# A planner that brings VectorE's planned time up to TensorE's at every unit of products

## The chip, the cores and the metric

The kernel runs on one core of a Trainium2 chip. Five engines work side by side on that core: TensorE (PE in the profile; PEld is its weight load), VectorE (DVE), ScalarE (ACT), GpSimd (POOL) and SyncE (SP), which here only issues transfers. Each engine has its own list of instructions, and semaphores make one wait for another. The metric is the device time of one execution in microseconds (us), lower is better; runs of the kernel before agree within 0.1%.

## The reference

The input goes through a block-wise linear attention with decay, then through two gated feed-forward layers. In short:

```python
for b in range(nb):                       # blocks of 64 positions
    intra = (qb @ kb.T * Dmask) @ vb
    inter = (qb * lam_pow) @ kv_state
    out[b] = intra + inter
    kv_state = lam_block * kv_state + (kb * rev_pow).T @ vb
x = out.reshape(1536, 512)
h = x @ w_in1;  x = (h * clip(h + 3, 0, 6) / 6) @ w_out1      # first layer, 512 -> 2048 -> 512
h = max(x @ w_in2, 0);  return (h * h) @ w_out2               # second layer, the same sizes
```

The four weight matrices arrive in 64-bit floating point; q, k, v and lam are 32-bit.

## The kernel before

**Tiles.** After the attention the 1536 tokens lie in three blocks of 512 (`j` = 0 to 2). The 2048 hidden features of a layer are 16 tiles of 128 (`f`), handled in four groups of four (`GROUP`). A *hidden unit* (`hidden`, called "h") multiplies one block by one tile of the input weights; a *projection unit* (`project`, called "y") multiplies a group's four hidden tiles of a block by the output weights for one quarter of the result, and adds the group's part to an accumulator. Every value is split into a high and a low part, so a product takes three matmuls: each unit is 12 matmuls of 128x512.

**The order of the units.** A list written at the end of the function sets it. For each layer, group and block it puts one hidden unit, then the four projection units of the block before, then the three other hidden units of the group. Around the change's place, in the second layer (`layer` 1), this reads: h of block 0 tile 4; four y of block 2, group 0; h of block 0 tiles 5, 6, 7; h of block 1 tile 4; four y of block 0, group 1; h of block 1 tiles 5, 6, 7.

**What follows a hidden unit in the second layer.** ScalarE reads the product `ph` from PSUM and applies Relu (L410), squares it (L411) and writes the high part `gh` (L412); VectorE subtracts that to get the low part `gl` (L414). (The slots of these two have other names for some tiles: `gkT` and `gk`, `gv` and `gq`, `gA`.) Three PSUM buffers hold `ph`, so a hidden unit can begin only when ScalarE has read the one three hidden units before. A projection unit takes the group's tiles in turn; the 12th of its matmuls takes the low part of the fourth tile. For group 0 the result is copied by ScalarE (L462); for later groups VectorE adds it to the accumulator (L465).

**Decoding of the weights.** A tile of 64-bit weights is fetched by SyncE into one of four `raw` buffers (L136). ScalarE takes a magnitude `da` (L145), VectorE then makes seven pieces of work: clamp (L160), shift (L164), join (L170), power (L177), lower (L181), rest (L186) and add (L189). After join ScalarE writes the high part (`wih` or `woh`, L173), for which rest waits; add writes the low part (`wil` or `wol`). There are seven places for decoded tiles of each kind, and a tile's place becomes free when its last product is done: for `w_out` of a group, after the last projection unit of block 2.

**The planner.** All engines' orders are those in which the Python code calls the instructions. The code keeps two planned times, `pe_t` for TensorE and `dve_t` for VectorE. A unit adds 2.72 to `pe_t` and then calls `decode_until(pe_t)`, which puts in pieces of decoding, at 0.44 or 0.7 each, until `dve_t` is 0.3 past `pe_t`. `vector(ready, cost)` does the same up to the time at which a piece of the products' own VectorE work is ready, and then counts that work; a subtraction `gl` of the second layer is called for `pe_t` + 2.4. Two things let `dve_t` stand still while `pe_t` goes on: `decode_piece` returns 0 when no place for a decoded tile is free, and a projection unit of group 0 calls no `vector`, since ScalarE copies its result.

Of the kernel before, what the change touches and what calls it, by code (L numbers as in the profile page):

```python
# [33 lines left out]
def decay_attention_moe_moe(  # L34
# [175 lines left out]
    pe_t, dve_t = 0.0, 0.0  # L210
    freed = []

    def decode_until(us):
        nonlocal dve_t
        while dve_t < us + LATE:
            cost = decode_piece()
            if not cost:
                return
            dve_t += cost
# [4 lines left out]
        dve_t = max(dve_t, ready) + cost  # L224

    def unit():
        nonlocal pe_t
        pe_t += UNIT
        decode_until(pe_t)

# [156 lines left out]
    def hidden(layer, j, f):  # L387

        n = BLOCKS[j] * P
        free_weights()  # L390
        wih, wil = weight(("wi", layer, f))
        ph = ps_h.tile([P, n], F32, tag="ph", name="ph")
        for a in range(KD):
            for i, (w, x) in enumerate(((wih, x_hi[j]), (wih, x_lo[j]), (wil, x_hi[j]))):
                nc.tensor.matmul(  # L395
                    ph, w[:, a * P : (a + 1) * P], x[:, a, :],
                    start=a == 0 and i == 0, stop=a == KD - 1 and i == 2,
                )
        if j == len(BLOCKS) - 1:
            freed.append(("wi", layer, f))  # L400
        unit()
        s, gh, gl = g_tiles()
        gh, gl = gh[:, :n], gl[:, :n]
        g = gp.tile([P, n], F32, tag="g", name="g")
        if layer == 0:
            nc.scalar.activation(g, ph, AF.Relu, bias=three)  # L406
            vector(pe_t + SCALAR, TWO)
            nc.vector.scalar_tensor_tensor(g, g, 6.0, ph, op0=ALU.min, op1=ALU.mult)  # L408
        else:
            nc.scalar.activation(g, ph, AF.Relu)  # L410
            nc.scalar.activation(g, g, AF.Square)  # L411
        nc.scalar.copy(gh, g)  # L412
        vector(dve_t + SCALAR if layer == 0 else pe_t + 3 * SCALAR, TWO)
        nc.vector.tensor_tensor(gl, g, gh.bitcast(F32), op=ALU.subtract)  # L414
        g_t[layer, j, f] = (gh, gl, s)
# [13 lines left out]
    def project_by_unit(layer, j, grp, f):  # L429

        n = BLOCKS[j] * P
        free_weights()
        if f == GROUP * grp:
            two = ps_s.tile([P, 2, n], F32, tag="sc", name="py2")
            py_t.update({e: two[:, e, :] if e < 2 else ps_y.tile([P, n], F32, tag="py", name="py") for e in range(KD)})
        for e in range(KD):
            products(layer, j, grp, e, f, py_t[e])
        unit()
        if f == GROUP * (grp + 1) - 1:
            for e in range(KD):  # L440
                project(layer, j, grp, e, py_t.pop(e))

    def project(layer, j, grp, e, py=None):
# [4 lines left out]
        if py is None:  # L448
            free_weights()
            py = ps_y.tile([P, w], F32, tag="py", name="py")  # L450
            for f in fs:
                products(layer, j, grp, e, f, py)
            unit()
# [67 lines left out]
    dve_t = 1.0  # L521
# [66 lines left out]
```

## Time and profile before

| | |
|---|---|
| median of 3 runs | 585.89 us (585.48 to 586.01) |
| the profiled execution | 587.42 us, of which its span 585.6 us |
| TensorE busy | 572.7 us, 98% of the span |
| VectorE busy | 420.4 us, 72% |
| ScalarE busy | 255.5 us, 44% |
| mean granted TensorE clock | 0.993 |

The span runs from the first to the last instruction; 1.8 us of the profiled execution lie around it. Engines overlap, so the shares don't add up. A TensorE instruction is shown with its whole passage through the array (0.39 us), while the next one starts 0.227 us after it: gaps are read from the starts. A number in square brackets behind a row of a timeline is how long the engine had been idle, and what ended that.

### The profile page before, as it was taken

How to read it: one execution, taken by the hardware profiler on the slowest of the kernel's cores; microseconds unless marked ns; L12 is line 12 of the kernel's file. 1: busy time of each engine (PE TensorE's matmuls, PEld its weight loads, DVE VectorE, ACT ScalarE, POOL GpSimd, SP SyncE). 2: the span in 40 equal slices, each digit the busy share in tenths (PEclk: the TensorE clock that was granted, in tenths of full speed). 3: DMA queues.
4: the chain of work that ended last, by engine and by line, in shares of the span. 5: the costliest groups of instructions: out<-in, count | busy, mean ns of one | idle time of the engine just before them, and what ended most of it. 6: DMA issues, size and time to landing. Idle time of an engine off the chain costs nothing.

```text
span 585.6 us, 7733 instructions
## 1 busy us (share of the span) xinstructions
PE 572.7 (98%) x3022; PEld 471.1 (80%) x3022; DVE 420.4 (72%) x723; ACT 255.5 (44%) x417; POOL 31.6 (5%) x36
## 2 busy tenths in 40 slices
PE   8899999999999999999999999988999999999997
PEld 5788888888888888888888888876888888888885
DVE  6789899989885899579988993379543998242222
ACT  1224555453441443344554774454522654532530
POOL 3782000000000000000000000000000000000000
PEclk9999999999999999999999999998999999999999
DMA  8982223332230232112221331113110320001011
GB/s 324 407 313 74 72 73 107 109 107 78 67 109 4 73 105 73 36 39 70 73 72 37 108 114 67 37 72 109 36 37 0 99 82 1 0 1 54 37 54 72
DMA packets 18035, 49.77 MB, mean 85 GB/s; under 512 B 2128, under 2 KB 2128, under 8 KB 18000
## 3 DMA queue, kind: packets, MB, share of 16 engines
q1 hardware_dynamic: 17856, 49.04, 24.0%
q8 instruction: 23, 0.38, 0.3%
q10 hardware_dynamic: 144, 0.26, 0.1%
q14 instruction: 12, 0.10, 0.1%
HBM read 46.14 MB, written 3.15 MB: 84 GB/s over the span
## 4 chain that ended last, share of the span: by engine, by line
PE 93%; DVE 3%; DMA 3%; ACT 0%; issue 0%; SPq 0%; DVEq 0%
PE py L427 45%; PE ph L395 43%; PE pxt L330 2%; PE psc L314 2%; PE pxt L355 1%; DMA lent<-in_qT 1%; DMA lent<-in_k 1%; PE pst L336 1%; DMA k<-in_k 1%; DVE du L186 0%; DVE da L181 0%; ACT da L145 0%; DVE du L170 0%; DVE wil L189 0%; DVE da L177 0%
## 5 line engine op out<-in xcount | busy, mean ns | idle before, releaser
L395 PE MATMUL ph<-xh,wih 128*128 128x512 f32 x384 | 149.6, 390 | 1.8 <-ACT g L410 1.8
L395 PE MATMUL ph<-xh,wil 128*128 128x512 f32 x384 | 149.4, 389 | 0.0
L395 PE MATMUL ph<-xl,wih 128*128 128x512 f32 x384 | 149.4, 389 | 0.0
L465 DVE TENSOR_TENSOR acc<-acc,py 128x512 f32<-128x512 f32 x72 | 49.3, 685 | 51.3 <-PE py L427 50.7
L395 PEld LDWEIGHTS ph<-xh,wih 128*128 128x128 f32 x384 | 72.1, 188 | 17.2 <-ACT g L410 2.2
L395 PEld LDWEIGHTS ph<-xh,wil 128*128 128x128 f32 x384 | 72.1, 188 | 15.0
L395 PEld LDWEIGHTS ph<-xl,wih 128*128 128x128 f32 x384 | 72.1, 188 | 15.0
L145 ACT ACTIVATE da<-raw 128x512 f32<-128x512 f32 x64 | 43.0, 674 | 42.4 <-DVE wol L189 22.5
L414 DVE TENSOR_TENSOR gl<-g,gh 128x512 fp32r<-128x512 f32 x48 | 33.0, 687 | 38.7 <-ACT gh L412 38.6
L410 ACT ACTIVATE g<-ph 128x512 f32<-128x512 f32 x48 | 28.6, 597 | 59.8 <-PE ph L395 59.8
L181 DVE SCALAR_TENSOR_TENSOR da<-raw,da 128x512 f32<-128x512 uint32 x64 | 44.6, 696 | 2.0
L170 DVE SCALAR_TENSOR_TENSOR du<-raw,da 128x512 int32<-128x512 int32 x64 | 44.3, 691 | 2.0
L173 ACT CAST woh<-du 128x512 fp32r<-128x512 f32 x32 | 19.8, 620 | 59.0 <-DVE du L170 59.0
L408 DVE SCALAR_TENSOR_TENSOR g<-g,ph 128x512 f32<-128x512 f32 x48 | 32.9, 685 | 14.5 <-ACT g L406 14.3
L412 ACT CAST gh<-g 128x512 fp32r<-128x512 f32 x48 | 29.9, 623 | 21.1 <-DVE g L408 20.4
L427 PE MATMUL py<-woh,gl 128*128 128x512 f32 x96 | 37.8, 394 | 0.0
L427 PE MATMUL py<-wol,gh 128*128 128x512 f32 x96 | 37.7, 392 | 0.0
L406 ACT ACTIVATE g<-ph,three 128x512 f32<-128x512 f32 x48 | 32.9, 686 | 10.8 <-PE ph L395 10.3
L427 PE MATMUL py<-woh,gh 128*128 128x512 f32 x96 | 37.6, 392 | 0.0
L427 PE MATMUL py<-gh,woh 128*128 128x512 f32 x96 | 37.3, 389 | 0.0
L427 PE MATMUL py<-gl,woh 128*128 128x512 f32 x96 | 37.3, 389 | 0.0
L427 PE MATMUL py<-gh,wol 128*128 128x512 f32 x96 | 37.3, 389 | 0.0
(94 smaller groups left out, 913.9 us busy)
## 6 DMA issues: line engine op xcount, KB each, us to landing
raw<-in_w_in SPq DMA_DIRECT2D x32, 512.0 KB, 3.2
raw<-in_w_out SPq DMA_DIRECT2D x32, 512.0 KB, 3.3
out<-acc SPq DMA_DIRECT2D x12, 256.0 KB, 2.0
kT<-in_kT SPq DMA_DIRECT2D x6, 256.0 KB, 5.2
k<-in_k SPq DMA_DIRECT2D x6, 256.0 KB, 5.1
v<-in_v SPq DMA_DIRECT2D x6, 256.0 KB, 5.3
lent<-in_kT SPq DMA_DIRECT2D x6, 256.0 KB, 5.4
lent<-in_qT SPq DMA_DIRECT2D x6, 256.0 KB, 5.4
```

The lines of the kernel that those rows point to most:

```text
L145: nc.scalar.activation(abs_t[n], raw_t[n][:, :, 1].bitcast(F32), AF.Abs, scale=2.0**16)
L170: nc.vector.scalar_tensor_tensor(u, hi32, -(2**31), ai, op0=ALU.bitwise_and, op1=ALU.bitwise_or)
L173: nc.scalar.copy(hi, u.bitcast(F32))
L181: nc.vector.scalar_tensor_tensor(a, lo32.bitcast(U32), 2.0**-52, a, op0=ALU.mult, op1=ALU.mult)
L395: nc.tensor.matmul(ph, w[:, a * P : (a + 1) * P], x[:, a, :], start=a == 0 and i == 0, stop=a == KD - 1 and i == 2,)
L406: nc.scalar.activation(g, ph, AF.Relu, bias=three)
L408: nc.vector.scalar_tensor_tensor(g, g, 6.0, ph, op0=ALU.min, op1=ALU.mult)
L410: nc.scalar.activation(g, ph, AF.Relu)
L412: nc.scalar.copy(gh, g)
L414: nc.vector.tensor_tensor(gl, g, gh.bitcast(F32), op=ALU.subtract)
L427: nc.tensor.matmul(py, a, b, start=f == fs[0] and i == 0, stop=f == fs[-1] and i == 2)
L465: nc.vector.tensor_tensor(t, t, py, op=ALU.add)
```

## The change

One line is added to `unit()`, which every hidden and projection unit calls once: before it adds the unit's 2.72 to `pe_t`, `dve_t` is raised to `pe_t` if it is below. Nothing else is edited; from there on the line numbers are one higher.

```diff
     def unit():
-        nonlocal pe_t
+        nonlocal pe_t, dve_t
+        dve_t = max(dve_t, pe_t)
         pe_t += UNIT
         decode_until(pe_t)
```

The orders of PE, POOL and SP are the same before and after. VectorE's and ScalarE's differ in one stretch, in the second layer, from the first hidden unit behind block 2's projection units of group 0 up to the projection units of block 1 in group 1. No instruction is added or left out.

VectorE before, at the start of that stretch: `wih3` and `wih4` are decoded input weights, `gl3` is the low part of block 0's tile 5. Ahead of the first row shown stand the whole decoding of `woh2`, and of `wih3` all but its last two pieces.

```order
L186 TENSOR_TENSOR du_3387<-du_3387,wih3_786 128x512
L189 TENSOR_TENSOR wil3_787<-du_3387,da_3376 128x512
L160 TENSOR_SCALAR da_3389<-da_3389 128x512
L164 TENSOR_SCALAR da_3389<-da_3389 128x512
L170 SCALAR_TENSOR_TENSOR du_3400<-raw_3188,da_3389 128x512
L177 TENSOR_SCALAR da_3389<-du_3400 128x512
L181 SCALAR_TENSOR_TENSOR da_3389<-raw_3188,da_3389 128x512
L186 TENSOR_TENSOR du_3400<-du_3400,wih4_1125 128x512
L189 TENSOR_TENSOR wil4_1126<-du_3400,da_3389 128x512
L160 TENSOR_SCALAR da_3402<-da_3402 128x512
L164 TENSOR_SCALAR da_3402<-da_3402 128x512
L414 TENSOR_TENSOR gl3_870<-g_3409,gh3_869 128x512
```

VectorE now, at the same place: `gl3`, `gk` and `gq` are the low parts of block 0's tiles 5, 6 and 7. Ahead of the first row stand the same decoding of `woh2` and the clamp and shift of `wih3`.

```order
L170 SCALAR_TENSOR_TENSOR du_3391<-raw_3110,da_3376 128x512
L415 TENSOR_TENSOR gl3_870<-g_3384,gh3_869 128x512
L177 TENSOR_SCALAR da_3376<-du_3391 128x512
L181 SCALAR_TENSOR_TENSOR da_3376<-raw_3110,da_3376 128x512
L186 TENSOR_TENSOR du_3391<-du_3391,wih3_786 128x512
L415 TENSOR_TENSOR gk_945<-g_3412,gkT_944 128x512
L189 TENSOR_TENSOR wil3_787<-du_3391,da_3376 128x512
L160 TENSOR_SCALAR da_3393<-da_3393 128x512
L164 TENSOR_SCALAR da_3393<-da_3393 128x512
L170 SCALAR_TENSOR_TENSOR du_3440<-raw_3188,da_3393 128x512
L415 TENSOR_TENSOR gq_1020<-g_3433,gv_1019 128x512
```

So `gl3` stands behind 10 pieces of decoding instead of 23, and three or four pieces stand between one low part and the next.

ScalarE before, behind the four copies of block 2's projection units: two magnitudes and two casts of input weights stand ahead of the Relu (L410) of block 0's tile 5.

```order
L173 CAST woh2_997<-du_3374 128x512
L145 ACTIVATE da_3389<-raw_3188 128x512
L173 CAST wih3_786<-du_3387 128x512
L145 ACTIVATE da_3402<-raw_3215 128x512
L173 CAST wih4_1125<-du_3400 128x512
L410 ACTIVATE g_3409<-ph_3361 128x512
L411 ACTIVATE g_3409<-g_3409 128x512
L412 CAST gh3_869<-g_3409 128x512
```

ScalarE now, at the same place (Relu is L411):

```order
L173 CAST woh2_997<-du_3374 128x512
L411 ACTIVATE g_3384<-ph_3361 128x512
L412 ACTIVATE g_3384<-g_3384 128x512
L413 CAST gh3_869<-g_3384 128x512
L145 ACTIVATE da_3393<-raw_3188 128x512
L173 CAST wih3_786<-du_3391 128x512
```

The Relu of tile 5 now comes ahead of these casts. The decoding of `wih4`, `wih5` and of `woh3` to `woh5` moves back in the same way, until the two orders meet again in the four additions (L465, now L466) of block 1 in group 1.

## Rows read from the trace of the kernel before

**Rows 1.** The page's first part: engines' busy time, share, instructions.

```profile
PE 572.7 (98%) x3022; PEld 471.1 (80%) x3022; DVE 420.4 (72%) x723; ACT 255.5 (44%) x417; POOL 31.6 (5%) x36
```

**Rows 2.** The chain that ended last: start, us, what it was.

```profile
337.99 10.88 PE ph L395 x48
...
370.63 10.89 PE py L427 x48
...
581.48 0.69 DVE acc L465
```

**Rows 3.** Timeline of PE, 370 to 410 us: start, us, instruction [idle before].

```profile
370.25 0.39 PE L395 MATMUL ph<-xh,wil 128*128 128x512 f32 x1
...
381.35 0.39 PE L395 MATMUL ph<-xh,wih 128*128 128x512 f32 x1
...
389.29 0.39 PE L395 MATMUL ph<-xh,wil 128*128 128x512 f32 x1
391.50 0.50 PE L395 MATMUL ph<-xh,wih 128*128 128x512 f32 x1 [1.82 <-ACT g L410]
...
395.95 0.39 PE L427 MATMUL py<-wol,gkT 128*128 128x512 f32 x1
397.26 0.50 PE L427 MATMUL py<-woh,gk 128*128 128x512 f32 x1 [0.92 <-DVE gk L414]
...
398.04 0.40 PE L427 MATMUL py<-wol,gv 128*128 128x512 f32 x1
399.26 0.50 PE L427 MATMUL py<-woh,gq 128*128 128x512 f32 x1 [0.82 <-DVE gq L414]
...
409.38 0.39 PE L395 MATMUL ph<-xh,wih 128*128 128x512 f32 x1
```

**Rows 4.** Windows: from:to, us, busy (instructions) by engine, granted clock, DMA share, GB/s.

```profile
25.40:27.30 1.90, 0.03 (x2) 0.00 (x0) 1.90 (x4) 1.10 (x2) 0.00 (x0) 1.00 1.02 402
27.30:31.80 4.50, 4.46 (x54) 3.90 (x56) 3.38 (x5) 0.00 (x0) 3.43 (x3) 0.62 1.05 403
...
399.80:403.50 3.70, 3.70 (x11) 2.89 (x10) 3.63 (x8) 1.11 (x3) 0.00 (x0) 0.54 0.40 117
```

**Rows 5.** Timeline of ACT, 366 to 412 us.

```profile
370.67 0.60 ACT L410 ACTIVATE g<-ph 128x512 f32<-128x512 f32 x1 [0.80 <-PE ph L395]
...
381.55 0.59 ACT L462 COPY acc<-py 128x512 f32<-128x512 f32 x1 [2.13 <-PE py L427]
...
382.60 0.61 ACT L173 CAST woh<-du 128x512 fp32r<-128x512 f32 x1
...
390.33 0.62 ACT L173 CAST wih<-du 128x512 fp32r<-128x512 f32 x1 [0.85 <-DVE du L170]
390.85 0.59 ACT L410 ACTIVATE g<-ph 128x512 f32<-128x512 f32 x1
```

**Rows 6.** Timeline of DVE, 340 to 412 us.

```profile
342.73 0.69 DVE L414 TENSOR_TENSOR gl<-g,gh 128x512 fp32r<-128x512 f32 x1
...
345.72 0.68 DVE L414 TENSOR_TENSOR gq<-g,gv 128x512 fp32r<-128x512 f32 x1
...
372.62 0.69 DVE L414 TENSOR_TENSOR gl<-g,gh 128x512 fp32r<-128x512 f32 x1 [2.03 <-ACT gh L412]
...
383.24 0.69 DVE L186 TENSOR_TENSOR du<-du,woh 128x512 f32<-128x512 f32 x1 [7.21 <-ACT woh L173]
...
384.64 0.42 DVE L160 TENSOR_SCALAR da<-da 128x512 f32<-128x512 f32 x1
...
388.69 0.42 DVE L160 TENSOR_SCALAR da<-da 128x512 f32<-128x512 f32 x1
...
393.52 0.68 DVE L414 TENSOR_TENSOR gl<-g,gh 128x512 fp32r<-128x512 f32 x1
...
398.52 0.68 DVE L414 TENSOR_TENSOR gq<-g,gv 128x512 fp32r<-128x512 f32 x1
```

**Rows 7.** DMA issues on the page: instructions, KB each, median us to landing.

```profile
raw<-in_w_out SPq DMA_DIRECT2D x32, 512.0 KB, 3.3
```

## The prediction

> **What bounds the kernel now.** I read the page's busy times first, then the chain of waits, then the timelines of TensorE, ScalarE and VectorE around the one place where the order changes, and the windows for the granted clock. TensorE is busy for 572.7 of 585.6 us, VectorE for 420.4 [rows 1]. The chain says the same: from the first hidden unit on it is made of pieces of TensorE, 10.88 us for 48 matmuls (0.2267 us each, 2.72 us a unit) [rows 2]. VectorE can thus cost time only where TensorE waits for it, and what the change is worth must be read at the stretch that it rearranges.
>
> That stretch is where the chain leaves TensorE. The 96 matmuls from the first of block 0's tile 5 (381.35) to the first of block 1's tile 5 (409.38) take 28.03 us [rows 3]; at 0.2267 each they would take 21.76. The loss is 6.27 us, and its parts are seen in the starts:
> - 389.29 to 391.50: the hidden unit of block 1 waits for ScalarE's Relu, which frees a `ph` buffer; 2.21 less a matmul's 0.23 is 1.98 us [rows 3].
> - 395.95 to 397.26: TensorE waits for VectorE's `gk`, the low part of tile 6; 1.08 us [rows 3].
> - 398.04 to 399.26: it waits for `gq`, that of tile 7; 0.99 us [rows 3].
> - 399.80 to 403.50: TensorE runs on, but the granted clock is 0.54, near the lower of its two levels; 3.70 times 0.46 is 1.70 us [rows 4].
> - The other 0.52 us are single intervals a little over 0.2267 behind each gap.
>
> Why it happens stands in the other two timelines. VectorE is idle for 7.21 us until 383.24, since the cast of `woh` that it waits for stands behind four copies on ScalarE, the last at 381.55 [rows 5, 6]. The planner counted no such standstill: its `dve_t` had stayed behind while no place was free and ScalarE did the copies, so it thought that VectorE had had those units for decoding, and put 23 pieces ahead of tile 5's low part. They run from 383.24 on without a pause, and the low part comes at 393.52 [rows 6]. ScalarE is drawn in: its Relu stands behind casts that wait for VectorE's join, the last at 390.33, and so begins at 390.85, though its matmuls began their last at 381.35 + 11 x 0.2267 = 383.84 [rows 3, 5].
>
> **The change part by part.** No instruction comes or goes, and TensorE's and the DMA queue's orders stay, so all of it is this one rearrangement. I carry it forward from the same 381.35.
>
> *The lag without a queue.* A last matmul at 370.25 is followed by the Relu at 370.67 and the low part at 372.62, 0.69 long [rows 3, 5, 6]. So a Relu follows by 0.42, and the low part by 1.95 more.
>
> *Tile 5.* Relu at 384.26: ScalarE is free, its cast of `woh` ends at 382.60 + 0.61 = 383.21 [rows 5]. Its low part would be ready at 386.2. VectorE has the clamp, shift and join of `wih3` ahead of it, from 384.64; seven pieces take 388.69 - 384.64 = 4.05 us, 0.58 each, so it is free at 386.4 [rows 6]. The low part begins there, against 393.52. The `ph` buffer is free at about 384.9, and the unit that waits for it comes at 381.35 + 3 x 2.72 = 389.51: the 1.98 us go.
>
> *Tile 6.* Its last matmul begins at 386.56, but now a magnitude and a cast stand ahead of its Relu, behind tile 5's high part (386.2): some 1.2 us by rows of 0.6 each [rows 5], so Relu at 387.4 and low part at 389.4. TensorE wants it as the 9th matmul of the unit at 392.23, at 394.04: 4 us in hand less the 0.7 that it takes. The 1.08 us go.
>
> *Tile 7.* Last matmul 389.28, Relu 389.7, ready at 391.6. VectorE has four pieces between the two low parts, 390.1 + 2.3 = 392.4, and ends at 393.1. It is wanted as the 12th matmul, 392.23 + 2.49 = 394.72: 1.6 us in hand. The 0.99 us go. This is the tightest place here.
>
> *What is late next.* The work put off is decoding, `wih4` and `wih5`, then `woh3` to `woh5`; those weights belong to group 2, which TensorE reaches only after two more rounds of 8 units, 40 us on, so their own lateness costs nothing. What it could cost is lateness of block 1's low parts, which before had VectorE almost to themselves. There, from 403.11 on, a low part (0.6) with four pieces (2.3) makes 2.9 us on VectorE for each unit of 2.72: it falls back 0.2 us a unit, 0.8 in four units, against 1.6 to 2.4 in hand. The trace has a near likeness: at 342.73 and 345.72 two low parts stand 2.99 us apart with four pieces of output weights between them, and TensorE's 48 matmuls from 337.99 still take 10.88 [rows 2, 6]. I take nothing for it. From below nothing can be gained there, since TensorE is at its pace already; from above it costs one gap like those seen, 0.99, and a clock fall of 1.70. A raw tile lands in 3.3 us [rows 7], less than the 4.05 of a decoding, and decodings now come at a slower pace, so I take nothing for that either.
>
> *The clock.* Twice in this trace TensorE stands nearly idle and then gets a low clock: 1.90 us idle at 25.40, then 0.62 for 4.50 us; the three gaps from 389.5 to 399.3, then 0.54 [rows 3, 4]. With no gaps I expect no fall, and the 1.70 us go too. Before the first of these falls the clock stayed at 1.00 during the idle time itself, so the fall comes late and not at a fixed distance. The Trainium skill ("TensorE: Matmul & The Clock Gate", What's actually happening) says that the chip judges activity in a window that runs on freely and isn't set back when a kernel starts. By that, the same gaps may bring a fall in one execution and none in another, and the gain in the median would lack that term, 581.3 in place of 579.6; the two falls in one trace neither show nor refute it.
>
> *The sum.* 1.98 + 1.08 + 0.99 + 1.70 + 0.52 = 6.27 us off. Everything behind 409.38 moves forward as a whole, with the last addition at 581.48 and the output behind it [rows 2]. The profiled execution would go from 587.42 to 581.15 (span 579.3). It was 1.53 us over the median of 585.89; I take the same 6.27 off that and get 579.6.
>
> **The rivals.**
> - *The clock fall is not in the timed runs, or stays.* For it: the profiled execution is 1.53 us over the median, about the price of one fall. Against: the three timed runs lie within 0.53 us, so none of them has a fall more or less than another, and both idle stretches in the trace were followed by one. Gain 6.27 - 1.70 = 4.57: 581.3.
> - *One gap stays.* VectorE comes over 1.6 us later to a group's fourth low part than worked out, in block 0 or block 1, and TensorE waits once, with a fall behind it: 6.27 - 0.99 - 1.70 = 3.6 off, 582.3. For it: pieces stand between all low parts now. Against: the likeness at 342.73.
> - *The stall moves.* VectorE's 7.21 us of idle time stay, and the same decoding must be done after them; if the backlog hits block 1 as it hit block 0, nothing is won: 585.9. Against: it is spread over some 40 us in which VectorE had idle time.
> - *Slower.* Decodings now stand between the low parts, so a raw tile that lands late holds every low part behind it. It decides when landing exceeds the time since the buffer was freed, by more than the 1.6 us in hand, on three decodings in a row: 3 x 3.3 - 1.6 = 8.3 of waiting and 1.70 of clock, less the 6.27 gained: 589.6. Against: the denser burst before ran from 383.24 to 393.52 with no wait for a transfer.
>
> **How the numbers follow.** Full gain 0.70, no gain from the clock 0.18, one gap stays 0.07, the stall moves 0.03, slower 0.02. A measurement tells about 0.2% (1.2 us) from no change. Faster: the first three, 0.95; same 0.03; slower 0.02. The predicted time is the first case's, 579.6. The range goes down to 578.8 for an idle interval or two that I count as unavoidable, and up to 582.0, past the clock's case and the edge of one gap.
>
> **What would show it.** In the profile after: no wait of TensorE for the Relu, `gk` or `gq` in that stretch; 96 matmuls from the same start in 21.8 us; the first low part some 5 us behind the start of its unit instead of 12; a granted clock of 1.00 there; VectorE's idle 7.2 us still there. It is wrong if TensorE waits for a low part in block 1, or if the clock falls with no gap ahead of it.

## The result, and the profile after

| | before | changed | ratio (95% interval) |
|---|---|---|---|
| recorded with the prediction | 585.95 us (585.48 to 586.36) | 581.10 us (579.96 to 581.28) | 0.9918 (0.9901 to 0.9935) |
| a second comparison | 585.03 us (584.16 to 587.76) | 580.91 us (579.96 to 582.29) | 0.9921 (0.9900 to 0.9942) |

The changed kernel is faster by 0.8%: 4.85 us by the first pair of medians, 4.12 by the second. The forecast was 579.6, so the way and the range were right, and the gain is 1.4 to 2.2 us smaller than the 6.27 worked out. One of the first executions of the changed kernel, the one that was profiled, took 1485.77 us, with matmuls of 512 columns 0.595 us apart in place of 0.227 and a recorded granted clock of 1.00, for a reason that nothing here shows; it stands in no number above, and the profile read here is that of the second comparison.

TensorE's waits as that profile lists them: engine and line, what it waited for, us in total, times, longest. (`psc` is the product of the attention's scores, `A` those scores with the decay, `pst` the product for the state; `warm` are matmuls ahead of the work.)

```profile
PE psc L315 <- DVE A L316: 3.6, 3, 2.0
PE warm L500 <- DVE idle L485: 1.2, 1, 1.2
PE pst L337 <- POOL kd L302: 0.2, 1, 0.2
```

The waits for `ph`, `gk` and `gq` [rows 3] are gone. What is left in the list lies ahead of the feed-forward layers, in a part that the change doesn't touch; and the last 48 matmuls of the chain take 11.44 us in place of 10.88, as they did before (11.43). The chain, in its middle part:

```profile
370.22 10.88 PE py L428 x48
381.10 10.88 PE ph L396 x48
391.98 10.88 PE py L428 x48
402.86 10.88 PE ph L396 x48
```

Where it left TensorE before, it now runs through. The first matmuls of block 0's tile 5 and of block 1's tile 5:

```profile
380.94 0.39 PE L396 MATMUL ph<-xh,wih 128*128 128x512 f32 x1
...
402.70 0.39 PE L396 MATMUL ph<-xh,wih 128*128 128x512 f32 x1
```

So the 96 matmuls between take 21.76 us, against 28.03 [rows 3]. VectorE at the same place:

```profile
382.82 0.69 DVE L186 TENSOR_TENSOR du<-du,woh 128x512 f32<-128x512 f32 x1 [7.21 <-ACT woh L173]
...
385.81 0.69 DVE L415 TENSOR_TENSOR gl<-g,gh 128x512 fp32r<-128x512 f32 x1
...
388.70 0.69 DVE L415 TENSOR_TENSOR gk<-g,gkT 128x512 fp32r<-128x512 f32 x1 [0.54 <-ACT gkT L413]
...
391.44 0.69 DVE L415 TENSOR_TENSOR gq<-g,gv 128x512 fp32r<-128x512 f32 x1
...
413.48 0.69 DVE L415 TENSOR_TENSOR gA<-g,gA 128x512 fp32r<-128x512 f32 x1
```

This execution is 0.41 us ahead of the earlier one at the first hidden unit of the stretch (380.94 against 381.35 [rows 3]). With that taken off, the prediction put the three low parts at 386.0, 389.0 and 392.0; they are at 385.81, 388.70 and 391.44. VectorE's 7.21 us of idle time stay [rows 6]. The last row is the low part of block 1's tile 7, which the prediction took for the next tight place: it ends at 414.17, and TensorE wants it for the 12th matmul of the unit that begins at 413.58, at 416.07.

The windows of that execution (the third number from the end is the granted clock: 1.00 is the upper of TensorE's two levels, 0.50 the lower):

```profile
28.00:31.50 3.50, 3.50 (x44) 2.94 (x44) 2.42 (x4) 0.00 (x0) 2.73 (x3) 0.55 1.06 406
...
380.00:390.00 10.00, 10.00 (x45) 8.26 (x44) 6.43 (x12) 7.01 (x13) 0.00 (x0) 1.00 0.14 43
390.00:425.00 35.00, 35.00 (x156) 29.00 (x155) 31.10 (x56) 17.50 (x29) 0.00 (x0) 1.00 0.28 93
```

The clock is 1.00 through the stretch, and the early low clock in the attention is still there.

### The profile page after: what moved, and what is told of

It is laid out like the page before. It is cut to its first block, busy times and chain, and to the rows that moved or that the text cites. A ratio compares the mean times of both kernels' runs of the same rounds, so it can differ in the third digit from the quotient of the medians.

```text
span 1483.6 us, 7734 instructions
## 1 busy us (share of the span) xinstructions
PE 1477.0 (100%) x3022; PEld 885.7 (60%) x3022; DVE 426.5 (29%) x723; ACT 256.6 (17%) x417; POOL 31.4 (2%) x36
## 4 chain that ended last, share of the span: by engine, by line
PE 100%; DVE 0%; issue 0%
PE py L428 46%; PE ph L396 46%; PE psc L315 2%; PE pxt L356 2%; PE pxt L331 2%; PE pst L337 1%; PE warm L500 1%; DVE A L316 0%; DVE acc L466 0%; DVE idle L485 0%
## 5 line engine op out<-in xcount | busy, mean ns | idle before, releaser
L396 PE MATMUL ph<-xh,wil 128*128 128x512 f32 x384 | 318.1, 828 | 0.0
L396 PE MATMUL ph<-xl,wih 128*128 128x512 f32 x384 | 318.0, 828 | 0.0
L396 PE MATMUL ph<-xh,wih 128*128 128x512 f32 x384 | 318.0, 828 | 0.0
L396 PEld LDWEIGHTS ph<-xl,wih 128*128 128x128 f32 x384 | 135.3, 352 | 93.4 <-issue 93.4
L396 PEld LDWEIGHTS ph<-xh,wih 128*128 128x128 f32 x384 | 135.0, 352 | 93.7 <-issue 93.7
L396 PEld LDWEIGHTS ph<-xh,wil 128*128 128x128 f32 x384 | 135.2, 352 | 93.2 <-issue 93.1
L466 DVE TENSOR_TENSOR acc<-acc,py 128x512 f32<-128x512 f32 x72 | 49.6, 688 | 369.6 <-PE py L428 369.6
L411 ACT ACTIVATE g<-ph 128x512 f32<-128x512 f32 x48 | 28.7, 598 | 323.7 <-PE ph L396 323.7
L428 PE MATMUL py<-gl,woh 128*128 128x512 f32 x96 | 79.7, 830 | 0.0
L428 PE MATMUL py<-gh,wol 128*128 128x512 f32 x96 | 79.5, 828 | 0.0
L428 PE MATMUL py<-gh,woh 128*128 128x512 f32 x96 | 79.5, 828 | 0.0
L428 PE MATMUL py<-woh,gA 128*128 128x512 f32 x64 | 52.7, 823 | 0.0
```

The lines of the kernel that those rows point to most:

```text
L396: nc.tensor.matmul(ph, w[:, a * P : (a + 1) * P], x[:, a, :], start=a == 0 and i == 0, stop=a == KD - 1 and i == 2,)
L428: nc.tensor.matmul(py, a, b, start=f == fs[0] and i == 0, stop=f == fs[-1] and i == 2)
L466: nc.vector.tensor_tensor(t, t, py, op=ALU.add)
```

## The experiments

**The changed kernel and the kernel before, once more.** No edit; they give traces and clocks to compare.

> The changed kernel once more, for a trace at full speed and for more timed runs. Theory A (the worked sum, with the clock's fall at 399.8 us of the kernel before as part of the gain): 579.6 us, no TensorE wait in the stretch from 381 to 404 us, 96 matmuls in 21.8 us there. Theory B (that clock fall is not in most timed runs of the kernel before, or an equal one comes in the changed kernel): 581.0 to 581.4, no wait in the stretch either, and the granted clocks of kernel before and changed kernel differ by less than 0.003. Theory C (a new gap in block 1's hidden units or in the projection units behind them): 581 to 582 and a TensorE wait for a low part somewhere from 390 to 425 us.

> The kernel before once more, for a second trace and for its clocks run by run. Theory A: a clock fall of about 3.7 us behind the gaps from 389 to 399 us again, mean clock 0.993, span 585.6. Theory B: the fall is absent or shorter in this execution, mean clock 0.995 to 0.996, and the gaps themselves (1.98, 1.08, 0.99 us) are there all the same.

The changed kernel, as shown: no wait in the stretch or right behind it, so the theory of a new gap falls. Its 580.91 us stand between what the other two said, 0.1 from theory B's 581.0 and 1.3 from theory A's 579.6; the mean clocks differ by 0.001 in the median (0.997 before, 0.996 now), as theory B has it. The kernel before took 585.72 us in its own timed runs here, and its second trace reads, for TensorE's waits and the clock:

```profile
390.02 0.50 PE L395 MATMUL ph<-xh,wih 128*128 128x512 f32 x1 [1.82 <-ACT g L410]
...
397.78 0.50 PE L427 MATMUL py<-woh,gq 128*128 128x512 f32 x1 [0.66 <-DVE gq L414]
```

```profile
390.00:394.00 4.00, 3.98 (x12) 3.17 (x13) 3.86 (x9) 3.82 (x7) 0.00 (x0) 0.65 0.37 131
394.00:398.00 4.00, 3.34 (x14) 2.46 (x13) 3.97 (x8) 3.72 (x7) 0.00 (x0) 0.92 0.42 131
398.00:403.00 5.00, 5.00 (x23) 4.07 (x23) 4.90 (x10) 1.99 (x4) 0.00 (x0) 1.00 0.34 108
```

The low clock came here too, but earlier: behind the first gap, not behind the last. The wait for `gk` is missing: TensorE, slowed, comes to it at 396.28, when `gk` has been done since 395.73. From 379.87 to 406.34 the 96 matmuls take 26.47 us, a loss of 4.71 and not 6.27. So the low clock that fell between the gaps was paid out of the waits that followed; the one behind the last gap [rows 4] came on top.

**Two steps between.** The edit, in the same line:

```diff
-        dve_t = max(dve_t, pe_t)
+        dve_t = max(dve_t, pe_t - 5.44)     # one kernel;  - 2.72 in the other
```

> Half of the change: VectorE's planned time is raised only to two units (5.44 us) behind TensorE's, so 17 pieces of decoding stand ahead of tile 5's low part (23 before, 10 after). Theory A, by the rows of before: the third magnitude now stands ahead of the Relu, at about 389.4, so the hidden unit at 389.5 waits some 0.5 us, and tile 7's low part comes about 1.1 to 1.3 us late; 1.8 us of gaps instead of 4.05, and a clock fall of up to 1.7 us: 581.5 to 583.5. A rival by which the gain comes from all of the stretch and not from the number of pieces ahead of the low part would give the changed kernel's time here too.

> VectorE's planned time is raised only to one unit (2.72 us) behind TensorE's: 14 pieces ahead of tile 5's low part. Theory A: low part of tile 5 at 388.2, the Relu ahead of the casts, tile 7's low part done at 394.1 against 394.7 when TensorE wants it: no gap, and the changed kernel's time within 0.3 us. If the slack worked out for tile 7 is too generous by 0.6 us or more, one gap of up to 0.5 us shows at the 12th matmul of the first projection unit.

Two units of lag: 583.05 us, ratio 0.9960 (0.9947 to 0.9974). Its trace has a wait for the Relu and waits for tile 7, where they were expected. Counted from the starts, as the prediction does, they are 0.51, 0.95 and 0.64 us, 2.1 in all against 1.8 expected. The expectation counted 17 pieces ahead of tile 5's low part; the trace has 19:

```profile
389.31 0.50 PE L396 MATMUL ph<-xh,wih 128*128 128x512 f32 x1 [0.34 <-ACT g L411]
395.33 0.50 PE L428 MATMUL py<-woh,gv 128*128 128x512 f32 x1 [0.68 <-ACT gv L413]
396.55 0.50 PE L428 MATMUL py<-woh,gq 128*128 128x512 f32 x1 [0.48 <-DVE gq L415]
```

The 96 matmuls take 24.42 us there (380.64 to 405.06), 2.66 over 21.76. One unit of lag: 580.86 us, ratio 0.9920 (0.9898 to 0.9943), no wait, 21.80 us. With 23, 19, 14 and 10 pieces ahead of tile 5's low part the loss is 4.7 (without the low clock), 2.66, 0.04 and 0: it hangs on the number of pieces. It ends at about the place that was worked out: with 14 pieces tile 7's low part begins at 393.62, ends at 394.30 and is wanted at 381.09 + 13.37 = 394.46.

**The Relu ahead of the casts.** In the kernel before, for one hidden unit alone, ScalarE's part is called ahead of the planner:

```diff
-        unit()
+        early = (layer, j, f) == (1, 0, 5)
+        if not early:
+            unit()
...
         nc.scalar.copy(gh, g)
+        if early:
+            unit()
```

> The kernel before, with one call moved: for block 0's tile 5 in the second layer ScalarE's Relu, square and cast are called ahead of the planner's decoding, so they no longer stand behind the casts of weights; VectorE keeps its 23 pieces ahead of the low part. Theory A (one lateness, that of VectorE's low parts, and the three gaps are where TensorE meets it): the wait for the ph buffer, 1.98 us, is gone, but the waits for low parts grow by as much, since tile 7's still comes some 4.5 us after it is wanted; time as the kernel before within 0.5 us. Rival (the ph wait is a cost of its own, by ScalarE's order): 2 us off, and the waits for gk and gq as before.

591.03 us, ratio 1.0093 (1.0076 to 1.0109): slower by 5.3 us, which neither had expected. The wait for the `ph` buffer is gone, as both said, and one long wait for the low part of tile 5 has taken its place. TensorE in this kernel:

```profile
397.22 0.79 PE L431 MATMUL py<-woh,gl 128*128 128x512 f32 x1 [4.78 <-DVE gl L418]
398.32 0.80 PE L431 MATMUL py<-woh,gkT 128*128 128x512 f32 x1 [0.31 <-ACT gkT L414]
...
400.21 0.80 PE L431 MATMUL py<-woh,gk 128*128 128x512 f32 x1 [0.67 <-DVE gk L418]
...
402.21 0.80 PE L431 MATMUL py<-woh,gq 128*128 128x512 f32 x1 [0.34 <-DVE gq L418]
```

ScalarE, and VectorE's first and last rows of the burst, tell why:

```profile
383.18 0.60 ACT L412 ACTIVATE g<-ph 128x512 f32<-128x512 f32 x1 [2.13 <-PE ph L395]
...
385.56 0.60 ACT L173 CAST woh<-du 128x512 fp32r<-128x512 f32 x1
```

```profile
386.19 0.69 DVE L186 TENSOR_TENSOR du<-du,woh 128x512 f32<-128x512 f32 x1 [11.26 <-ACT woh L173]
...
396.48 0.68 DVE L418 TENSOR_TENSOR gl<-g,gh 128x512 fp32r<-128x512 f32 x1
```

Tile 7's low part on VectorE, and the windows (here with TensorE's busy time alone ahead of the granted clock):

```profile
401.47 0.69 DVE L418 TENSOR_TENSOR gq<-g,gv 128x512 fp32r<-128x512 f32 x1
```

```profile
392.40:397.20 4.80, 0.04 (x1) 0.82 0.46 166
397.20:402.20 5.00, 3.67 (x6) 0.50 0.35 106
402.20:405.00 2.80, 2.79 (x7) 0.50 0.04 4
```

The Relu waits until 383.18 for its matmuls, and the cast of `woh`, with which VectorE's burst begins, now stands behind it. This execution is 1.09 us ahead of the one with [rows 3], so the burst begins 386.19 - (383.24 - 1.09) = 4.04 us later, is as long as before (10.29 against 10.28 [rows 6]), and all low parts come 4 us later: tile 7's at 401.47, which is 4.04 behind 398.52 - 1.09. The stretch takes 32.10 us, 4.07 more than the 28.03 of [rows 3]; both have a low clock behind their last gap, here 0.50 from 397.2 to 405. So the whole stretch moved by VectorE's 4.04, though the 1.98 us for the `ph` buffer were gone. The theory of one lateness holds in its main point, and the `ph` wait was no cost of its own. The "within 0.5 us" was wrong because I moved one instruction in ScalarE's queue without asking who waits for the one behind it.

**Raised past TensorE's time.**

```diff
-        dve_t = max(dve_t, pe_t)
+        dve_t = max(dve_t, pe_t + 1.36)
```

> VectorE's planned time is raised to half a unit (1.36 us) past TensorE's at every unit. Theory A: TensorE has no wait left in the stretch, so raising further gains nothing, and it thins out decoding in the first layer, where the plan has little to spare: the changed kernel's time within 0.3 us, or up to 2 us above it if a weight comes late. A rival by which the change gives slack that more of it would widen: faster than the changed kernel.

588.42 us, ratio 1.0048 (1.0025 to 1.0071): slower than before, and by 7.5 us than the changed kernel, far past the 2 us allowed for. The stretch of the change is whole here (21.76 us); the loss is in the first layer, where a decoded weight comes late, first its high part and then its low part:

```profile
PE ph L396 <- ACT wih L173: 3.3, 1, 3.3
PE ph L396 <- DVE wil L189: 1.6, 1, 1.6
```

The last of the pieces through which the chain runs from 122.33 to 130.59:

```profile
119.58 2.73 PE ph L396 x12
122.31 0.02 issue
...
129.25 0.61 DVE du L186
129.86 0.02 issue
129.88 0.70 DVE wil L189
130.59 0.04 issue
130.63 8.11 PE ph L396 x22
```

In the first layer, VectorE has two pieces of its own for each hidden unit beside the decoding. A plan that counts it as busy half a unit longer can put in too little, and by the code `weight()` then puts in the rest at once. The trace shows the late weight; this cause is read from the plan alone.

**The attention's gap.** Both kernels have the wait for `A` near 25 us, behind the first three pieces of decoding, and in some executions a low clock behind it. The attention is worked in 12 chunks, and `ATT_FILL` is the decoding that the plan puts into each. Two edits try to take the wait away: to begin that decoding a chunk later (in the changed kernel and in the kernel before), and to call ScalarE's first magnitude a chunk sooner (in the changed kernel).

```diff
-        if c >= 3:
-            owed += ATT_FILL
+        if c >= 4:
+            owed += ATT_FILL * 9 / 8
```

```diff
         state_values(c)
+        if c == 2:
+            magnitude(0)
```

> The changed kernel, with the decoding inside the attention begun one chunk later and its amount kept (9/8 as much a chunk). The kernels so far all show TensorE idle for about 1.9 us near 25 us, behind the first three pieces of decoding, and in some executions a low clock behind it. Theory A (a low clock comes only behind gaps): both go, 1.9 us and the low clock's share, so 578 to 579, and the timed executions spread by less than 1 us, all at a mean clock of 0.998 or more. Rival (the low clock at 28 us comes of itself): 579 to 580, with a low clock in as many executions as before. If the gap only moves a chunk later, 580.9 as the changed kernel.

> The kernel before, with only the decoding in the attention begun one chunk later, as in the run beside it, so the early gap should be gone and the gaps of 389 to 399 us stay. Theory A: the difference to the changed kernel with the same edit is what the change is worth where no early clock fall confuses it: 4.6 us by the gaps, a little more in executions with a low clock at 391 to 403 us. Expected 582.5 to 583.5. Rival (the late low clock is a cost on top of the gaps in every execution): the difference is 6 us or more.

Neither gained, and both missed what was expected: 581.69 us and 586.07. VectorE in the changed kernel with the later start still waits for its first magnitude, one chunk on:

```profile
26.95 0.65 DVE L160 TENSOR_SCALAR da<-da 128x512 f32<-128x512 f32 x1 [1.57 <-ACT da L145]
```

But the pair gives the change's worth beside one another: 586.07 - 581.69 = 4.38 us. And the trace of the kernel before with that edit is the one with all three gaps and no low clock at all in the stretch:

```profile
391.10 0.50 PE L395 MATMUL ph<-xh,wih 128*128 128x512 f32 x1 [1.82 <-ACT g L410]
396.86 0.50 PE L427 MATMUL py<-woh,gk 128*128 128x512 f32 x1 [0.89 <-DVE gk L414]
398.86 0.50 PE L427 MATMUL py<-woh,gq 128*128 128x512 f32 x1 [0.82 <-DVE gq L414]
```

```profile
396.00:400.00 4.00, 2.32 (x8) 1.45 (x9) 3.90 (x9) 3.72 (x7) 0.00 (x0) 1.00 0.41 131
400.00:404.00 4.00, 4.00 (x20) 3.29 (x19) 3.97 (x8) 1.12 (x2) 0.00 (x0) 1.00 0.39 135
```

From 380.96 to 407.38 its 96 matmuls take 26.42 us: a loss of 4.66 by the gaps alone.

> The changed kernel, with one call more inside the attention: ScalarE's first magnitude of a weight is called one chunk sooner (after chunk 2), so VectorE need not stand 1.57 us idle ahead of its first three pieces of decoding, which delay the score mask behind which TensorE stands idle for 1.9 us near 25 us. Theory A (a low clock follows gaps): the gap shrinks by about 1.5 us and the low clock near 28 us goes in most executions: 578.5 to 579.5. Rival (transfers, not VectorE, set that stage's pace): the gap is found again a chunk later and the time is the changed kernel's, 580.9 within 0.5.

578.47 us (578.24 to 578.79), ratio to the kernel before 0.9885 (0.9866 to 0.9904): faster than both. VectorE's first piece now comes without a wait, and TensorE waits 2.2 us for `A` in place of 3.6:

```profile
21.69 0.42 DVE L160 TENSOR_SCALAR da<-da 128x512 f32<-128x512 f32 x1
```

```profile
PE psc L315 <- DVE A L316: 2.2, 3, 1.3
```

All four timed executions had a mean clock of 0.999 or more and lie within 0.6 us. The first layer begins at 49.67 us in this trace and at 51.75 in that of the changed kernel.

**And the last group's end.** The kernel just told of, with one line that moves the fourth projection unit of block 1 behind block 2's last hidden units:

```diff
+    units.append(units.pop(-len(fs) - 1))
     units += [("y", l, j, g, e) for e in range(ny(l, j))]
```

> The kernel of the run beside it, and in the last group of the second layer the fourth projection unit of block 1 moved behind the three last hidden units of block 2, so TensorE need not wait for the low part of the very last tile (two waits of about 0.1 and 0.2 us, 0.55 us with what follows them). 0.5 us below the run beside it if that wait is as independent as it looks; the same time if it only moves.

578.26 us (577.89 to 579.97), ratio 0.9886 (0.9868 to 0.9903). The last 60 matmuls of the chain take 13.61 us, their plain pace, where the last 48 of its neighbour take 11.44 in place of 10.88, so the wait is gone. The 0.5 us expected didn't come: the 0.2 us between the medians can't be told from no change.

## Why the prediction was right, and where its sum was off

*The mechanism.* Right, step by step: no TensorE wait in the stretch, the three low parts within 0.6 us of their worked times, 7.21 us of VectorE's idle time left, no new lateness in block 1. Tile 7's low part has 2.2 us in hand (it ends at 392.13 and is wanted at 380.94 + 13.37 = 394.31), where 1.6 were worked out; the kernel with 14 pieces leaves 0.16 of it. One reading was wrong, without effect on the sum: five of the 23 pieces ran ahead of VectorE's idle time, from 373.23 on, and only 18 from 383.24. No run takes away the 7.21 us themselves, for example by calling the cast of `woh` ahead of the four copies, so whether that alone would do is open.

*The gaps.* 1.98 + 1.08 + 0.99 + 0.52 = 4.57 us were summed. Without a low clock they measure 4.66. They are not three costs: in the kernel with the Relu first the first of them is gone, and the stretch is longer by 4.07 us, just about the 4.04 by which VectorE began later. They add up because each is the part by which VectorE's lateness had grown since the one before.

*The clock, the term that was mis-sized.* The sum counted 1.70 us for the low clock at 399.80 [rows 4], since "both idle stretches in the trace were followed by one". In the kernel before's three traces of this stretch (the two of the same kernel and the one with the later fill) it comes once behind the gaps (28.03 us), once between them (26.47) and once not at all (26.42). What it adds is thus 1.6, 0.05 and 0.

Over 60 timed executions of the kernel before in the later comparisons, 15 had a mean clock of 1.000 and spans of 583.0 to 583.2 us, 28 had 0.997 and spans of 582.2 to 584.6, and only 5 had the 0.993 of the profile shown, with spans of 585.8 to 586.1: the profile on which I summed was of the longest kind. Their times run from 584.0 to 588.0, so the 0.1% by which runs were said to agree held for the first three alone. The sum then took the loss of this one execution off the median of others. The rival with the clock (581.3), which was given a chance of 0.18, was the nearer number, and its evidence, an execution 1.53 us over the median, was the better evidence; that the three timed runs lay within 0.53 us said nothing on whether they had the fall. The measured time lies in the range only because the range was drawn up past that rival's case. The rule of the Trainium skill ("TensorE: Matmul & The Clock Gate", What's actually happening), that the chip's window runs on freely, agrees with these three traces: the same lateness of VectorE, and the low clock behind the gaps, among them or nowhere.

*What is left between 4.1 and 4.85.* The early low clock in the attention comes in some executions of either kernel. In the second comparison 4 of the 6 executions of the changed kernel had a mean clock of 0.996, where its trace shows that low clock, and 8 of the 23 of the kernel before had 1.000. Its instructions up to there are the same, so I take this for chance; nothing here shows it to be more. Between executions at 0.999 or above, the spans are 583.0 to 583.2 before, against 578.6 for the changed kernel (one execution) and 578.4 and 578.6 for the one with a unit of lag: 4.4 to 4.8 us, about the gaps. The mean clock doesn't settle a span by itself: 11 of the 28 executions at 0.997 are shorter than all 15 at 1.000, and why is open.

*The rivals.* "One gap stays", "the stall moves" and "slower" are out by the trace of waits.

## What to carry to other kernels

Where a planner keeps a planned time for each engine, let an engine's time go on while it can't be given work; here the plan otherwise poured in work later for time that was gone, ahead of what others waited for. Raise it to now and no further: a unit less was as good here, half a unit more cost 7.5 us elsewhere. And before a term is taken from one profile, ask whether that execution is the usual one: its own time against the median says so.

## What the runs showed of the hardware that I had not expected

- The gaps of TensorE in the stretch are followed by the low clock in one execution, have it among them in another (where two of the three waits are left), and go without it in a third. Behind the last gap it cost 1.6 us; among them 0.05, since TensorE would have waited anyhow.
- In the kernel with the Relu first the clock fell while TensorE stood idle: it is 0.82 in the mean from 392.40 to 397.20, where no matmul starts until 397.22, and 0.50 behind. In the stretch of the kernel before it fell behind the gaps, with TensorE running [rows 4].
- In the attention VectorE's shift took 1.17 us beside a running GpSimd instruction, and 0.43 where none ran (rows of the changed kernel):

```profile
22.91 1.24 POOL L302 TENSOR_TENSOR kd<-k,decay 128x512 f32<-128x512 f32 x1
23.27 1.17 DVE L164 TENSOR_SCALAR da<-da 128x512 int32<-128x512 int32 x1
...
384.69 0.43 DVE L164 TENSOR_SCALAR da<-da 128x512 int32<-128x512 int32 x1
```

It ends 0.3 us after that instruction does. The Trainium skill ("SBUF — State Buffer", Terms, the entry on the shared port pair) says that VectorE and GpSimd hold a pair of ports in turn for a whole instruction; these rows agree, and no run here takes the cause apart.
